# Batch 0's pooled values multiplied unsummed on TensorE, and the second weight's rounded copies placed by the planner

## The chip, the cores and the metric

The kernel runs on one core of one Trainium2 chip. The metric is the device time of one execution in microseconds (us). A core has TensorE (PE, matrix products), VectorE (DVE), ScalarE (ACT), GpSimd (POOL) and SyncE (SP), which here issues all DMA transfers in one in-order queue. Each engine works through its own list of instructions in order and waits on semaphores for the others.

## The reference

Attention on 8 batches of 8 heads (576 positions, head size 64), and then a two-layer MLP over its 4608 rows of 512 numbers. The attention is a sum of two parts:

```python
q_d = q.reshape(B, H, Sd, factor, D).mean(axis=3)     # factor 4: 576 -> 144 positions
k_d = k.reshape(B, H, Sd, factor, D).mean(axis=3)
v_d = v.reshape(B, H, Sd, factor, D).mean(axis=3)
out_up = np.repeat(sm_attn(q_d, k_d, v_d), factor, axis=2)
mask = np.abs(pos[:, None] - pos[None, :]) < factor   # each position and 3 on both sides
out_local = softmax(where(mask, scale * q @ k.T, -1e9)) @ v
x = (out_up + out_local)                              # as 4608 x 512
h = x @ w_in                                          # 512 x 2048
return np.maximum(0.01 * h, h) @ w_out                # 2048 x 512
```

## The kernel before

**MLP.** Every product is made of three fp32r matmuls: each operand is split into a rounded copy (`xh`, `gh`, `wih`, `woh`) and the rest (`xl`, `gl`, `wil`, `wol`), and high x high, high x low and low x high are added up. The 4608 rows go in 13 chunks: 256 and 320 columns (batch 0), then mostly 384. For each of 16 blocks f of 128 hidden units, `up_proj` (L706) forms h of the chunk in a PSUM bank `hp`, `leaky` makes `gh` and `gl` out of it (L716 and L717 on ACT, L719 on DVE; the last one frees the bank, of which there are two), and `down_proj` (L746) adds it into four banks `acc`. The two chunks of batch 0 are done with blocks 0 to 7 first, and with blocks 8 to 15 when those weights are there.

**Weights.** `convert(f, k)` stages a block of `w_in` (k = 0) or `w_out` (k = 1), which arrives as 64-bit floats: a load into a buffer that is borrowed from the attention (`k`, `v`, `prod`, `up` and others), ACT extracts the top bits (L268), DVE puts the fp32 value together (L270), a rounded copy is made (L278 on DVE for k = 1, L281 on ACT for k = 0), and POOL subtracts it from the value (L283). Then the buffer is free for the next load.

**Attention.** Heads go in pairs c = 0 to 3. `pooled(b, c)` sums four rows of q and k (L345 on DVE for b = 0, c = 0, else L339 and L341 on POOL for batch 0), scores them on PE (L358), makes the softmax (L366 to L378), transposes it on PE (L397), and multiplies it with the summed values `v_d` (L409), which DVE sums out of `vs` (L387). The result is copied to `outd` by ACT (L414). For batch 0 the local part is done on PE by `banded` in windows of 70 keys, in two halves hf: scores L460 and L468, softmax L475 to L487, transposes L495, values L509. L521 adds the pooled part, L526 and L528 write `xh` and `xl`. For the other batches the local part is made on POOL and DVE (`scores`, `values`: L567, L573, L628, L634) and transposed on PE (L665) by `landing`.

**Order.** Nothing is scheduled on the chip: a planner in the kernel's Python code (`Order`) decides the order of every engine's instructions while the program is built. Each piece of work is a generator with a rank; it asks for buffers (`slot`), waits for named events (`wait`), and hands in operations with an engine and a size (`op`, `pe`, `load`). The planner keeps a time for each engine in `od.engine`, gives every operation a cost (`COST`: a fixed part and a part per element; PE's is given in us), and always records the operation that could start earliest, ties by rank. So every change of a cost moves instructions of all engines. Buffers named `su_...` exist for batch 0 only: `su_vs` holds four, one for the values `vs` of each head pair, and the windows of the second half of `banded` are loaded into the same four when they are free again. `su_vd` holds the sums of batch 0, two buffers.

Of the kernel before, what the change touches and what calls it, by code (L numbers as in the profile page):

```python
# [6 lines left out]
F32 = mybir.dt.float32  # L7
# [7 lines left out]
ALU = mybir.AluOpType  # L15
AX = mybir.AxisListType
PSUM = bass.MemoryType.PSUM

B, H, S, D = 8, 8, 576, 64
FAC = 4  # L20
SD = S // FAC
# [15 lines left out]
HEADS = 2  # L37
# [145 lines left out]
def attn_moe(ctx: ExitStack, tc, qkt, vd, qb, kb, vb, vwb, band, identb, w_in, w_out, ident, edge, out):  # L183
    nc = tc.nc
# [2 lines left out]
    wk = ctx.enter_context(tc.tile_pool(name="wk", bufs=1))  # L187
    ps = ctx.enter_context(tc.tile_pool(name="ps", bufs=1, space=PSUM))

    bufs = dict(head=HEADS, qk=1, vs=1, qk_d=2, v_d=1, su_vd=2, su_half=1, su_pd=3, su_ptd=2, st_d=3, pd=2, ptd=1, outd=2, q=1, k=1, v=1, s=3, st_l=3, prod=2, up=1,  # L190
                xloc=2, lst=3, gh=3, gl=3, o=2, hp=2, pt=2, xh0=1, xl0=1, xh1=1, xl1=1, acc0=1, acc1=1, acc2=1, acc3=1,
                su_vw=NC, su_vs=NC, su_pt=2)
    od = Order(bufs)
# [1 line left out]
    def slot(*tags):  # L195
        return (yield ("slot", tags, 0))

    def sb(s, shape, dtype, pool=None):
        tag = s.tag
        return (pool or wk).tile(shape, dtype, name=tag, tag=tag, bufs=bufs[tag])  # L200
# [4 lines left out]
    def op(eng, n, *after, times=1):  # L205
        if eng == "PE":
            dur = n
        else:
            a, k = COST[eng]
            dur = times * a + k * n  # L210
        return (yield ("op", eng, dur, max((0.0,) + after), 0, after))

    def pe(us, *after):
        return (yield ("op", "PE", us, max(after) + SAFE, 0))
# [40 lines left out]
    def convert(f, k):  # L255
        s = yield from slot(*(("k", "v", "prod", "up") if f < OWN else ("v", "up", "vs")), *(("xh1", "xl1") if f < 4 else ()))
        st = sb(s, [128, HALFS * (DM + 1)], U16)
        raw = st[:, 1:1 + HALFS * DM]
        if k == 0:
            t = yield from load(raw.rearrange("p (c m) -> p c m", c=NC), w_in_v[:, f], 524e3, s.t)  # L260
        else:
            t = yield from load(raw, w_out_v[:, f], 524e3, s.t)
        mid = st.bitcast(I32).rearrange("p (m w) -> p m w", w=2)[:, :DM, 1]
        top = st.rearrange("p (m h) -> p m h", h=HALFS)[:, 1:, 0].bitcast(BF16)
        s_u = yield from slot("head")
        head = heads[s_u.index % len(heads)]
        t = yield from op("ACT", 790, t, s_u.t)
        nc.scalar.copy(out=head.bitcast(F16).rearrange("p (m h) -> p m h", h=2)[:, :, 1], in_=top)  # L268
        t = yield from op("DVE", 780, t)
        nc.vector.scalar_tensor_tensor(out=mid, in0=mid, scalar=13, in1=head, op0=ALU.logical_shift_right, op1=ALU.bitwise_or)  # L270
        s_u.free(t)
        tf = mid.bitcast(F32)
        if f >= FSPLIT:
            yield from wait("late")
        hi, lo = (w.rearrange("p c m -> p (c m)") for w in weight(f, k))
        if k:
            t = yield from op("DVE", 512, t)
            nc.vector.tensor_copy(out=hi, in_=tf)  # L278
        else:
            t = yield from op("ACT", 512, t)  # L280
            nc.scalar.copy(out=hi, in_=tf)  # L281
        t = yield from op("POOL", 590, t)
        nc.gpsimd.tensor_tensor(out=lo, in0=tf, in1=hi.bitcast(F32), op=ALU.subtract)  # L283
        s.free(t)
        od.signal(("w", f, k), t)

    outd = {}
# [42 lines left out]
    def pooled(b, c, rank, pool=None):  # L330
        sq, sv, qk, vs, tq, tv = yield from fetch(b, c, pool)
        s_qd = yield from slot("qk_d")
        qk_d = sb(s_qd, [128, 2 * SD], F32)
        qkr = qk.rearrange("p a (s r) -> p (a s) r", r=FAC)
        if b < BANDED and (b, c) != (0, 0):
            s = yield from slot("su_half")
            half = sb(s, [128, 2 * SD, 2], F32, pool)
            t = yield from op("POOL", 576, tq, s.t, s_qd.t)
            nc.gpsimd.tensor_tensor(out=half, in0=qkr[:, :, :2], in1=qkr[:, :, 2:], op=ALU.add)  # L339
            t = yield from op("POOL", 288, t)  # L340
            nc.gpsimd.tensor_tensor(out=qk_d, in0=half[:, :, 0], in1=half[:, :, 1], op=ALU.add)  # L341
            s.free(t)
        else:
            t = yield from op("DVE", 1152, tq, s_qd.t)
            nc.vector.tensor_reduce(out=qk_d, in_=qkr, axis=AX.X, op=ALU.add)  # L345
        if sq:
            if b < BANDED:
                od.spawn(rank, keeper(b, c, sq, t))
            else:
                sq.free(t)  # L350
        s_st, s_pd = (yield from slot("st_d")), (yield from slot("su_pd" if pool else "pd"))
        s_b = yield from slot(*banks(b))
        sc = bank(s_b)
        t = yield from pe(0.9, t, s_b.t)
        for qi in range(3):
            for p in range(2):
                rows = slice(64 * p, 64 * p + 64)
                nc.tensor.matmul(sc[rows, qi * SD:(qi + 1) * SD], qk_d[rows, qi * QB:qi * QB + 64],  # L358
                                 qk_d[rows, SD:2 * SD], start=True, stop=True)
        s_qd.free(t)  # L360
        scv = sc[:, :3 * SD].rearrange("p (a s) -> p a s", a=3)
        st, pd = sb(s_st, [128, 2, 3], F32), sb(s_pd, [128, 3, SD], F32, pool)
        mx, rc = st[:, 0], st[:, 1]
        top, sm = sc[:, 3 * SD:3 * SD + 3], sc[:, 3 * SD + 4:3 * SD + 7]
        t = yield from op("DVE", 440, t, s_st.t, times=3)
        nc.vector.tensor_reduce(out=top, in_=scv, axis=AX.X, op=ALU.max)  # L366
        nc.vector.tensor_scalar(out=mx, in0=top, scalar1=-SCALE / (FAC * FAC), scalar2=None, op0=ALU.mult)  # L367
        t = yield from op("ACT", 432, t, s_pd.t, times=8)
        for qi in range(3):
            nc.scalar.activation(out=pd[:, qi], in_=scv[:, qi], func=AF.Exp, scale=SCALE / (FAC * FAC),  # L370
                                 bias=mx[:, qi:qi + 1], accum_out=sm[:, qi:qi + 1])
        t = yield from op("DVE", 10, t, times=4)
        nc.vector.tensor_scalar(out=rc, in0=sm, scalar1=1e-9, scalar2=float(FAC), op0=ALU.add, op1=ALU.mult)
        nc.vector.reciprocal(out=rc, in_=rc)
        s_b.free(t)
        if b < BANDED:
            t = yield from op("POOL", 432, t)
            nc.gpsimd.tensor_tensor(out=pd, in0=pd, in1=rc.unsqueeze(2).to_broadcast([128, 3, SD]), op=ALU.mult)  # L378
        else:
            t = yield from op("ACT", 432, t, times=5)  # L380
            for qi in range(3):
                nc.scalar.activation(out=pd[:, qi], in_=pd[:, qi], func=AF.Copy, scale=rc[:, qi:qi + 1])
        s_st.free(t)
        s_vd = yield from slot("su_vd" if pool else "v_d")
        v_d = sb(s_vd, [72, 2, 2, D], F32, pool)
        td = yield from op("DVE", 1050, tv, s_vd.t)
        nc.vector.tensor_reduce(out=v_d, in_=vs, axis=AX.X, op=ALU.add)  # L387
        if sv:
            sv.free(td)
        s_pt = yield from slot("su_ptd" if pool else "ptd")  # L390
        ptd = sb(s_pt, [72, 2, 2, 3, QB], F32, pool)
        for kc in range(2):
            s_b = yield from slot(*banks(b))
            tp = bank(s_b)
            tt = yield from pe(0.27, t, s_b.t)
            for qi in range(3):
                nc.tensor.transpose(tp[0:72, qi * 128:(qi + 1) * 128], pd[:, qi, kc * 72:kc * 72 + 72], id_sb)  # L397
            te = yield from op("ACT", 288, tt, s_pt.t)
            nc.scalar.copy(out=ptd[:, kc].rearrange("k p a q -> k a p q"),
                           in_=tp[0:72, :384].rearrange("k (a p q) -> k a p q", a=3, p=2)[:, :, :, :QB])  # L400
            s_b.free(te)
        s_pd.free(tt)
        to = yield from wait(("outd", b))
        s_b = yield from slot(*banks(b))
        av = bank(s_b)
        t = yield from pe(0.68, te, td, s_b.t)
        for p in range(2):
            for kc in range(2):
                nc.tensor.matmul(av[64 * p:64 * p + 64, :SD], v_d[:, p, kc], ptd[:, kc, p],  # L409
                                 start=kc == 0, stop=kc == 1)  # L410
        s_pt.free(t)
        s_vd.free(t)
        t = yield from op("ACT", 144, t, to)
        nc.scalar.copy(out=outd[b][:, c], in_=av[:, :SD])  # L414
        s_b.free(t)
        od.signal(("pooled", b, c), t)
        if b == 0:
            od.signal("su", t)
# [470 lines left out]
```

## Time and profile before

| | |
|---|---|
| median of 3 runs | 961.01 us (960.36 to 964.61) |
| profiled execution | 959.72 us, its span 957.9 us |
| mean granted PE clock | 0.996 |
| PE busy | 932.4 us, 97% of the span |
| DVE, ACT, POOL busy | 595.2, 415.0, 617.8 us |
| first MoE matmul starts | 44.19 us |

A span runs from the first to the last instruction. Busy times count an engine's own instructions; loads of weights into PE are counted apart, since they overlap matmuls. A row of a timeline or of the chain of waits begins with its start and its length; "x8" counts instructions. An fp32 matmul (not fp32r) stands in the trace as two instructions, called passes here. "<-" in brackets names the work that ended a wait.

### The profile page before, as it was taken

How to read it: one execution, taken by the hardware profiler on the slowest of the kernel's cores; microseconds unless marked ns; L12 is line 12 of the kernel's file. 1: busy time of each engine (PE TensorE's matmuls, PEld its weight loads, DVE VectorE, ACT ScalarE, POOL GpSimd, SP SyncE). 2: the span in 40 equal slices, each digit the busy share in tenths (PEclk: the TensorE clock that was granted, in tenths of full speed). 3: DMA queues.
4: the chain of work that ended last, by engine and by line, in shares of the span. 5: the costliest groups of instructions: out<-in, count | busy, mean ns of one | idle time of the engine just before them, and what ended most of it. 6: DMA issues, size and time to landing. Idle time of an engine off the chain costs nothing.

```text
span 957.9 us, 16170 instructions
## 1 busy us (share of the span) xinstructions
PE 932.4 (97%) x6282; PEld 894.8 (93%) x6282; DVE 595.2 (62%) x895; ACT 415.0 (43%) x1139; POOL 617.8 (64%) x356
## 2 busy tenths in 40 slices
PE   6799999999999999999999999999999999999997
PEld 5588999899999999999999999899999999999997
DVE  5986678888887776787657774862753753311111
ACT  3774555555545543445324553532513423422211
POOL 3759868777888778986798776884885873100000
PEclk9899999999999999999999999999999999999999
DMA  9755665644554523452424442431231220000000
GB/s 264 241 184 181 214 201 179 189 164 145 188 166 122 190 96 116 131 187 95 135 74 146 159 148 101 140 116 58 92 116 58 91 77 31 34 1 1 34 1 33
DMA packets 63180, 117.31 MB, mean 122 GB/s; under 512 B 4944, under 2 KB 32848, under 8 KB 63104
## 3 DMA queue, kind: packets, MB, share of 16 engines
q1 hardware_dynamic: 63104, 116.29, 38.6%
q8 instruction: 49, 0.80, 0.4%
q14 instruction: 27, 0.22, 0.1%
HBM read 105.65 MB, written 10.62 MB: 121 GB/s over the span
## 4 chain that ended last, share of the span: by engine, by line
PE 77%; POOL 8%; DMA 4%; issue 4%; DVE 4%; ACT 2%; SPq 0%; POOLq 0%; DVEq 0%; ACTq 0%
PE hp L706 35%; PE acc L746 34%; POOL prod L567 4%; POOL prod L628 3%; PE pt L358 2%; DMA k<-in_kb_dram 2%; PE pt L397 2%; PE pt L409 2%; PE pt L665 1%; DMA qk<-in_qkt_dram 1%; DVE s L573 1%; DMA v<-in_w_in_dram 0%; SPq L218 0%; DMA vs<-in_w_out_dram 0%; DVE gl L719 0%
## 5 line engine op out<-in xcount | busy, mean ns | idle before, releaser
L567 POOL TENSOR_TENSOR prod<-q,k 128x1344 f32<-128x1344 f32 (+1 forms) x88 | 266.3, 3027 | 81.3 <-DMA k<-in_kb_dram 55.2
L628 POOL TENSOR_TENSOR prod<-v,s 128x1344 f32<-128x1344 f32 (+1 forms) x88 | 265.6, 3021 | 32.3 <-DVE xloc L634 18.2
L706 PE MATMUL hp<-xh,wih 128*128 128x384 f32 (+2 forms) x832 | 279.9, 336 | 5.8 <-DVE gl L719 5.1
L746 PE MATMUL acc<-gh,woh 128*128 128x384 f32 (+2 forms) x832 | 274.4, 330 | 0.3 <-ACT o L780 0.3
L706 PE MATMUL hp<-xl,wih 128*128 128x384 f32 (+2 forms) x832 | 269.5, 324 | 0.3 <-DVE xl L680 0.3
L706 PE MATMUL hp<-xh,wil 128*128 128x384 f32 (+2 forms) x832 | 269.6, 324 | 0.0
L746 PE MATMUL acc<-gh,wol 128*128 128x384 f32 (+2 forms) x832 | 269.0, 323 | 0.0
L746 PE MATMUL acc<-gl,woh 128*128 128x384 f32 (+2 forms) x832 | 268.9, 323 | 0.0
L719 DVE TENSOR_TENSOR gl<-hp,gh 128x384 fp32r<-128x384 f32 (+2 forms) x208 | 108.5, 522 | 215.7 <-ACT hp L717 215.2
L716 ACT ACTIVATE gh<-hp 128x384 fp32r<-128x384 f32 (+2 forms) x208 | 97.3, 468 | 315.6 <-PE acc L746 307.9
L706 PEld LDWEIGHTS hp<-xh,wih 128*128 128x128 f32 x832 | 156.4, 188 | 15.6 <-DVE gl L719 8.0
L746 PEld LDWEIGHTS acc<-gh,woh 128*128 128x128 f32 x832 | 156.2, 188 | 4.0 <-issue 3.2
L706 PEld LDWEIGHTS hp<-xl,wih 128*128 128x128 f32 x832 | 156.7, 188 | 0.5 <-DVE xl L680 0.5
L706 PEld LDWEIGHTS hp<-xh,wil 128*128 128x128 f32 x832 | 156.4, 188 | 0.0
L746 PEld LDWEIGHTS acc<-gl,woh 128*128 128x128 f32 x832 | 156.3, 188 | 0.0
L746 PEld LDWEIGHTS acc<-gh,wol 128*128 128x128 f32 x832 | 156.2, 188 | 0.0
L573 DVE TENSOR_REDUCE s<-prod 128x21 f32<-128x1344 f32 (+1 forms) x88 | 130.2, 1479 | 27.9 <-POOL prod L567 27.9
L634 DVE TENSOR_REDUCE xloc<-prod 128x192 f32<-128x1344 f32 (+1 forms) x88 | 130.1, 1478 | 22.5 <-POOL prod L628 22.1
L717 ACT ACTIVATE hp<-hp 128x384 f32<-128x384 f32 (+2 forms) x208 | 96.1, 462 | 0.0
L672 DVE TENSOR_TENSOR pt<-pt,up 128x384 f32<-128x384 f32 (+1 forms) x44 | 37.8, 861 | 27.6 <-PE pt L665 22.2
L652 ACT COPY up<-outd 128x576 f32<-128x576 f32 x84 | 52.3, 675 | 0.0
L370 ACT ACTIVATE pd<-pt,st_d 128x144 f32<-128x144 f32 x84 | 32.1, 382 | 46.4 <-DVE st_d L367 35.4
(154 smaller groups left out, 754.3 us busy)
## 6 DMA issues: line engine op xcount, KB each, us to landing
k<-in_kb_dram SPq DMA_DIRECT2D x38, 576.0 KB
v<-in_vb_dram SPq DMA_DIRECT2D x38, 576.0 KB
qk<-in_qkt_dram SPq DMA_DIRECT2D x32, 576.0 KB
vs<-in_vd_dram SPq DMA_DIRECT2D x28, 288.0 KB
q<-in_qb_dram SPq DMA_DIRECT2D x38, 192.0 KB
out_dram<-o SPq DMA_DIRECT2D x36, 192.0 KB
v<-in_w_out_dram SPq DMA_DIRECT2D x4, 512.0 KB
prod<-in_w_out_dram SPq DMA_DIRECT2D x4, 512.0 KB
```

The costliest lines, as they stand in the source:

```text
L370: nc.scalar.activation(out=pd[:, qi], in_=scv[:, qi], func=AF.Exp, scale=SCALE / (FAC * FAC), bias=mx[:, qi:qi + 1], accum_out=sm[:, qi:qi ...
L567: nc.gpsimd.tensor_tensor(out=prv, in0=q[:, p, a - j0:z - j0].unsqueeze(2).to_broadcast([128, n, W, D]), in1=view(k[:, p], (a - j0) * D, [ ...
L573: nc.vector.tensor_reduce(out=s[:, p, a - j0:z - j0], in_=prv, axis=AX.X, op=ALU.add)
L628: nc.gpsimd.tensor_tensor(out=prv, in0=view(v[:, p], a - j0, [[1, n], [nv, D], [1, W]]), in1=s[:, p, a - j0:z - j0].unsqueeze(2).to_broadc ...
L634: nc.vector.tensor_reduce(out=xl_t[:, :n, p], in_=prv, axis=AX.X, op=ALU.add)
L652: nc.scalar.copy(out=up[:, pp], in_=outd[b][:, 2 * u + pp].unsqueeze(2).to_broadcast([128, SD, FAC]))
L672: nc.vector.tensor_tensor(out=xv, in0=xv, in1=upv, op=ALU.add)
L706: nc.tensor.matmul(hp[:, :n], wt[:, c], x[:, c], start=k == 0, stop=k == 3 * NC - 1)
L716: nc.scalar.activation(out=gh[:, :n], in_=hp[:, :n], func=AF.Prelu, alpha=0.01)
L717: nc.scalar.activation(out=hp[:, :n], in_=hp[:, :n], func=AF.Prelu, alpha=0.01)
L719: nc.vector.tensor_tensor(out=gl[:, :n], in0=hp[:, :n], in1=gh[:, :n].bitcast(F32), op=ALU.subtract)
L746: nc.tensor.matmul(acc[:, :n], wt[:, es], g[:, :n], start=f == f0 and j == 0, stop=f == f1 - 1 and j == 2)
```

## The change

In `pooled`, for batch 0 alone, the sum over four rows of v (L387, 72 x 1024 values to 72 x 256) is left out. The product L409 takes v as it lies in `vs`, once for each of the four rows r, with the same scores: 2 x 4 matmuls for each of the two heads instead of 2, and the two heads, whose outputs are the two halves of a bank's partitions, now take turns. The stationary operand is `vs[:, p, kc, :, r]`, 64 columns that lie four fp32 apart. `vs` is given back after the matmuls instead of after the sum; `su_vd` is no longer there. In `convert` the engine of the rounded copy is chosen by the planner's times, for both weights, instead of by k.

```diff
@@ convert
-        if k:
+        if max(od.engine["DVE"], t) + 0.4 < max(od.engine["ACT"], t):
             t = yield from op("DVE", 512, t)
             nc.vector.tensor_copy(out=hi, in_=tf)
         else:
             t = yield from op("ACT", 512, t)
             nc.scalar.copy(out=hi, in_=tf)
@@ pooled
-        s_vd = yield from slot("su_vd" if pool else "v_d")
-        v_d = sb(s_vd, [72, 2, 2, D], F32, pool)
-        td = yield from op("DVE", 1050, tv, s_vd.t)
-        nc.vector.tensor_reduce(out=v_d, in_=vs, axis=AX.X, op=ALU.add)
-        if sv:
+        if pool:
+            td = tv
+        else:
+            s_vd = yield from slot("v_d")
+            v_d = sb(s_vd, [72, 2, 2, D], F32)
+            td = yield from op("DVE", 1050, tv, s_vd.t)
+            nc.vector.tensor_reduce(out=v_d, in_=vs, axis=AX.X, op=ALU.add)
             sv.free(td)
...
-        t = yield from pe(0.68, te, td, s_b.t)
-        for p in range(2):
-            for kc in range(2):
-                nc.tensor.matmul(av[64 * p:64 * p + 64, :SD], v_d[:, p, kc], ptd[:, kc, p],
-                                 start=kc == 0, stop=kc == 1)
+        t = yield from pe(2.2 if pool else 0.68, te, td, s_b.t)
+        steps = [(kc, vs[:, :, kc, :, r]) for kc in range(2) for r in range(FAC)] if pool else [(kc, v_d[:, :, kc]) for kc in range(2)]
+        for n, (kc, vk) in enumerate(steps):
+            for p in range(2):
+                nc.tensor.matmul(av[64 * p:64 * p + 64, :SD], vk[:, p], ptd[:, kc, p], start=n == 0, stop=n == len(steps) - 1)
         s_pt.free(t)
-        s_vd.free(t)
+        (sv if pool else s_vd).free(t)
```

`pool` is set for batch 0 only. Lines below the change have numbers that are 2 higher in the changed kernel, L397 and what follows it up to L409 too; L409 becomes L412, and L414 becomes L416.

The planner's order changes on every engine. On PE, around the first set of value products (head pair 0), before:

```order
L358 MATMUL acc_188<-qk_d 64x144 x6
L409 MATMUL hp<-su_ptd,su_vd 64x144 x4
L509 MATMUL pt<-su_pt,su_vw 64x64 x8
L460 LDWEIGHTS idb_sb
L460 MATMUL acc_239<-band_sb,idb_sb 128x280
L468 MATMUL acc_239<-qk_91 64x67 x2
L468 MATMUL acc_239<-qk_91 64x70 x6
L495 MATMUL acc_226<-id_sb,xloc 70x128 x3
```

and after:

```order
L358 MATMUL acc_187<-qk_d 64x144 x6
L412 MATMUL hp<-su_ptd,su_vs 64x144 x16
L497 MATMUL acc_235<-id_sb,xloc 70x128 x3
L511 MATMUL acc_251<-su_pt,su_vw 64x64 x8
L358 MATMUL pt<-qk_d 64x144 x6
L497 MATMUL acc_264<-id_sb,xloc 70x128
L462 LDWEIGHTS idb_sb
L462 MATMUL hp<-band_sb,idb_sb 128x280
```

The set has 16 matmuls instead of 4; behind it now stand transposes of pair 1, and the window product of pair 0 (L509, now L511) has moved behind them.

On ACT, the first rounded copies of both weights (`wih`, `woh`; the name behind the arrow is the borrowed buffer), before:

```order
L268 CAST head_71<-v 128x512
L399 COPY su_ptd<-acc_359 72x3x2x48
L479 ACTIVATE xloc<-xloc 128x280
L497 COPY su_pt<-pt 70x384
L399 COPY su_ptd<-acc_384 72x3x2x48
L497 COPY su_pt<-acc_392 70x128
L268 CAST head_70<-prod 128x512
```

and after:

```order
L268 CAST head_70<-prod 128x512
L401 COPY su_ptd<-pt 72x3x2x48
L528 CAST xh_83<-hp 128x256
L281 CAST woh_68<-v 128x512
L499 COPY su_pt<-pt 70x384
L401 COPY su_ptd<-acc_362 72x3x2x48
L281 CAST wih_66<-prod 128x512
```

All 16 copies of `woh` have moved from DVE's list to ACT's, and none of either weight stands on DVE.

On SP, the first loads of weights (`k`, `v`, `prod`, `up`, `xh_102` are the borrowed buffers) and the first window load into `su_vs`, before:

```order
L218 DMA k<-in_w_in_dram 128x4x512
L218 DMA su_vs<-in_vwb_dram 70x640
L218 DMA v<-in_w_out_dram 128x2048
L218 DMA prod<-in_w_in_dram 128x4x512
L218 DMA prod<-in_w_out_dram 128x2048
L218 DMA up<-in_w_in_dram 128x4x512
```

and after:

```order
L218 DMA k<-in_w_in_dram 128x4x512
L218 DMA v<-in_w_out_dram 128x2048
L218 DMA prod<-in_w_in_dram 128x4x512
L218 DMA prod<-in_w_out_dram 128x2048
L218 DMA su_vs<-in_vwb_dram 70x640
L218 DMA up<-in_w_in_dram 128x4x512
L218 DMA xh_102<-in_w_out_dram 128x2048
L218 DMA xl_103<-in_w_in_dram 128x4x512
L218 DMA vs<-in_w_in_dram 128x4x512
```

The window load has moved three weight loads back; four weight loads stand between it and the next one.

More of the change, by code (lines that the diff above doesn't have):

```diff
@@ L188, in attn_moe @@
     ps = ctx.enter_context(tc.tile_pool(name="ps", bufs=1, space=PSUM))
-    bufs = dict(head=HEADS, qk=1, vs=1, qk_d=2, v_d=1, su_vd=2, su_half=1, su_pd=3, su_ptd=2, st_d=3, pd=2, ptd=1, outd=2, q=1, k=1, v=1, s=3, st_l=3, prod=2, up=1,
+    bufs = dict(head=HEADS, qk=1, vs=1, qk_d=2, v_d=1, su_half=1, su_pd=3, su_ptd=2, st_d=3, pd=2, ptd=1, outd=2, q=1, k=1, v=1, s=3, st_l=3, prod=2, up=1,
                 xloc=2, lst=3, gh=3, gl=3, o=2, hp=2, pt=2, xh0=1, xl0=1, xh1=1, xl1=1, acc0=1, acc1=1, acc2=1, acc3=1,
```

## The prediction

> **What bounds the kernel now.** I read the page's first part, then the same busy times by stage, then what TensorE (PE) waited for, then the chain of waits. The first part says that PE carries the time:
>
> ```profile
> PE 932.4 (97%) x6282; PEld 894.8 (93%) x6282; DVE 595.2 (62%) x895; ACT 415.0 (43%) x1139; POOL 617.8 (64%) x356
> ```
>
> The span of 957.9 us is therefore 932.4 us of PE work and 25.5 us in which PE sat idle. An edit can move the span only by changing one of these two. The table by stage (us of the stage, busy us of each engine with the number of instructions, granted clock, DMA share) says where the idle lies:
>
> ```profile
> core 0: us, PE busy (x) PEld busy (x) DVE busy (x) ACT busy (x) POOL busy (x), PEclk, DMA share, GB/s
> 0.00:20.00 20.00, 11.99 (x110) 9.34 (x111) 8.83 (x21) 6.72 (x23) 7.23 (x13) 1.00 0.92 251
> 20.00:44.00 24.00, 18.25 (x229) 13.34 (x231) 22.76 (x44) 18.52 (x53) 16.50 (x14) 0.86 0.93 289
> 44.00:70.00 26.00, 23.73 (x253) 22.30 (x248) 23.20 (x41) 18.99 (x44) 16.36 (x12) 1.00 0.56 174
> 70.00:130.00 60.00, 58.01 (x439) 55.98 (x438) 40.44 (x61) 31.73 (x78) 46.21 (x31) 1.00 0.64 200
> 130.00:200.00 70.00, 68.34 (x561) 63.97 (x560) 60.23 (x103) 39.05 (x125) 55.69 (x34) 1.00 0.57 179
> 200.00:640.00 440.00, 439.44 (x2911) 418.70 (x2910) 324.10 (x466) 206.77 (x601) 356.57 (x191) 1.00 0.43 137
> ...
> 770.00:958.00 188.00, 182.95 (x1050) 182.17 (x1048) 44.56 (x69) 49.07 (x112) 28.09 (x15) 1.00 0.08 27
> ```
>
> PE idles 8.0 us before 20, 5.75 from 20 to 44 (attention of batch 0), 2.3 from 44 to 70, 2.0 from 70 to 130, 1.7 from 130 to 200, 0.6 in the next 440 us, and 5.05 in the last stage, the tail. VectorE (DVE) is 95% busy from 20 to 44 and 89% from 44 to 70; nowhere later is it short. What PE waited for agrees:
>
> ```profile
> PE hp L706 <- DVE gl L719: 5.1, 10, 1.4
> PE acc L495 <- POOL xloc L487: 2.1, 1, 2.1
> PE acc L397 <- POOL su_pd L378: 2.0, 2, 1.3
> PE pt L509 <- ACT su_pt L497: 1.8, 1, 1.8
> PE pt L409 <- ACT su_ptd L399: 0.8, 2, 0.5
> ```
>
> (us in all, times, longest.) The 5.1 us are waits for a hp bank that DVE frees late. Ahead of the L509 wait, which ends at 38.2, and of the first MoE matmul (L706) at 44.2 the chain of waits stands on DVE; these are its longest piece there and the piece that ends the batch's first 256 columns, and two rows of PE's timeline:
>
> ```profile
> 35.36 1.75 DVE up L270
> 42.41 0.41 DVE xl L528
> 26.55 0.52 PE L397 MATMUL acc<-id_sb,su_pd 128*72 128x128 f32 x3 [0.71 <-POOL su_pd L378]
> 44.19 0.39 PE L706 MATMUL hp<-xh,wih 128*128 128x256 f32 x1
> ```
>
> The L495 wait, three us earlier, ends on GpSimd (POOL), which had waited for DVE's reciprocals. So both waits are DVE's.
>
> **The change: work taken off DVE.** The four sums of batch 0 go, and the sixteen rounded copies of the second weight (L278) leave DVE:
>
> ```profile
> L387 DVE TENSOR_REDUCE su_vd<-su_vs x4: 1183/1194/1205, 11.4 to 29.0; 72x256 f32<-72x1024 f32 x4
> sum 110.00, DVE 14.30; mean DVE 4.77
> L278 DVE CAST woh<-vs x2: 1374/1814/2254, 88.0 to 108.2; 128x512 fp32r<-128x512 f32 x2
> L281 ACT CAST wih<-v x4: 662/672/680, 45.6 to 106.4; 128x512 fp32r<-128x512 f32 x4
> ```
>
> The first row is 4 x 1.19 = 4.8 us, the second the sum of L278's busy time from 20 to 130 us. In the new order all 16 copies, and the 16 of the first weight as before, stand on ScalarE (ACT); DVE gets none, so "ACT or VectorE" is ACT alone. At ACT's 0.67 us (last row, same shape) that is 10.7 us more for ACT, off PE's path while ACT has room: it is 77% busy from 20 to 44 and 73% from 44 to 70.
>
> **Work put on PE.** Each head pair of batch 0 gets 16 matmuls instead of 4; the trace counts two passes for each fp32 matmul, so 32 instead of 8. The chain gives the pace:
>
> ```profile
> 16.48 1.17 PE hp L409 x8
> 14.85 1.64 PE acc L358 x12
> 609.96 0.65 PE pt L409 x8
> 611.86 0.88 PE pt L358 x12
> ```
>
> These are start, us on the chain, and passes. After 20 us a pass of the same shape takes 81 ns (0.65/8); a pass of L358, with the same 144 columns, but whose two column halves take turns as in the new loop, takes 73 ns (0.88/12). In the first 20 us PE is slower, with 146 and 137 ns, though the granted clock reads 1.00. I take L358's pace for its alternation. Three pairs at full pace: 32 x 0.073 - 0.65 = 1.7 us each, 5.1 in all; the first pair, at about 16.5 us: 32 x 0.137 - 1.17 = 3.2. Sum +8.3 us; by L409's own pace it is +9.4. All of it is PE time and nothing hides it except an idle PE. Behind the first set in PE's queue stand the transposes of pair 1, the window product of pair 0 and the scores of pair 2, all pushed by 3 us.
>
> **What idle it can fall into.** The 8.0 us before 20 are first loads and the first softmax, which the change doesn't shorten. Of the 5.75 from 20 to 44, the two DVE-made waits (2.1 and 1.8) should go, since DVE sheds three sums (3.6 us) and four copies (4.2) there, and 0.5 of the small ones: -4.4 (ends 0 and -5.75). These waits also cost clock:
>
> ```profile
> 30.48 0.69 PE L509 MATMUL acc<-su_pt,su_vw 70*64 70x64 f32 x16
> 38.23 1.12 PE L509 MATMUL pt<-su_pt,su_vw 70*64 70x64 f32 x16 [1.79 <-ACT su_pt L497]
> 39.68 1.42 PE L468 MATMUL hp<-qk 64*64 64x70 f32 x20
> 43.44 0.83 PE L468 MATMUL pt<-qk 64*64 64x70 f32 x20
> ```
>
> Equal work took 0.43 and 0.59 us longer right after the gaps, in the stage whose clock is 0.86: -1.0 with the gaps gone (ends 0 and -2). From 44 to 130 PE idles 4.3 us, mostly for gl. DVE is relieved by 10 us there, but gh and hp, which gl needs, now queue behind ACT's copies. I take 1.0 of 4.3 (ends +4.3 and -4.3). After 130 the work is the same and only the order differs: 0, give or take 1.7, the idle of 130 to 200.
>
> **The load queue.** A buffer of v is now given back by the matmuls instead of by DVE. SP issues loads in order, and the window load that reuses it stands ahead of weight loads; now it issues at
>
> ```profile
> 12.58 0.33 SPq L218 DMA_DIRECT2D su_vs<-in_vwb_dram  x1
> ```
>
> and then it would wait until the first set of matmuls ends, 16.5 + 4.4, about 21 us. Four weight loads stand behind it. I cost it at nothing: the DMA share is 0.92 and 0.93 up to 44 us, so the engines are still working off what was issued before. If that cover were gone, the price would be the weights coming 3 us later, against the first MoE matmul at 44.
>
> **Sum.** +8.3 - 4.4 - 1.0 - 1.0 = +1.9 us. Against the profiled execution's 959.72 that is 961.6. That execution lies 1.3 below the median of 961.01; I add half of it and say 962.2. A difference under 0.5% (4.8 us) is no change here.
>
> **Rivals.** *Faster: the idle was the real price.* For it speaks that DVE ends most waits up to 130 us. If all of 20 to 44 (5.75), the clock (1.0), the 4.3 of 44 to 130 and the 1.7 of 130 to 200 go, and the denser PE has reached full pace by the first set (its 3.2 becomes 1.7), the sum is +6.8 - 12.75 = -6 us, about 954.4. Against it: static orders on five engines never fit so well, and PE's first wait after 20 us is the 0.71 at 26.55 (row above), and two of the four sets fall ahead of it, where no idle can take them.
>
> *Slower: the strided operand.* The new stationary operand takes every fourth fp32 of v, 16 bytes apart; every stationary operand of L409 before was contiguous. If a pass had to wait for its own weight load, it would take that load's time:
>
> ```profile
> L409 PEld LDWEIGHTS pt<-ptd,v_d x224: 132/137/137, 128.5 to 633.8; 72*64 72x64 f32 x112
> L409 PEld LDWEIGHTS hp<-su_ptd,su_vd x8: 181/228/230, 16.4 to 17.0; 72*64 72x64 f32 x8
> ```
>
> That is 3 x (32 x 0.137 - 0.65) + 32 x 0.228 - 1.17 = +17.3, and less the 6.4 regained +10.9: 971.3. It passes 0.5% once a pass takes over some 92 ns at full pace (and 1.87 times that in the first set, the ratio of 137 to 73). Against it: loads overlap passes now (137 ns against a pace of 81), so some slack exists. The Trainium skill, "SBUF — State Buffer", section "Door 1: The DMA port swizzle", says that SBUF has 16-byte lines and that an access which goes to a new line each time pays a penalty; here every weight would be on a new line, so the page stands on this rival's side. No row of this trace has such an operand, and the page gives no figure.
>
> *Slower: ACT becomes what DVE was.* From 44 to 70 ACT is busy 18.99 of 26; some 8 of the copies before the first eight weight pairs are done bring 5.4 us, which makes 94%, above DVE's 89% now. If that doubles the 4.3 us of idle instead of saving 1.0, the sum is +1.9 + 1.0 + 4.3 = +7.2: 967.6. Against it: a copy took up to 2.25 us on DVE (row above) and 0.68 at most on ACT, so the chain for each weight is not longer.
>
> **Chances.** Forecast 0.60 (own range 958 to 966), all idle regained 0.19, strided operand 0.10, ACT 0.11. I leave out the strided case and the last of the fast one: 955 to 968.5. Faster 0.19, same 0.61, slower 0.20.
>
> **What would show it.** Right: L412 in 32 passes of about 73 ns after 20 us and about 4.4 us for the first set; PE busy up by 7 to 9 us; PE idle from 20 to 44 down to 1 or 2 us with the clock near 1; DVE 19 us lighter, ACT 10.7 heavier. Wrong: passes over 92 ns; new waits of PE for gh or gl while ACT copies; SP standing at the window load while the DMA engines run dry; or PE at full pace before its first set.

## The result, and the profile after

The changed kernel takes 970.3 us (median of 19 runs, 962.88 to 979.91), the kernel before 960.45 in the runs beside them: a ratio of 1.0089, 95% interval 1.0076 to 1.0102, or +8.5 us. (The averages, 969.3 and 960.8 us, give this ratio; the medians lie 9.9 us apart.) The forecast was 962.2, range 955 to 968.5. Ratios here and below leave out slow executions: 979.91 here, and two far ones among the experiments, 1859 us (products alone in the old order) and 4951 us (additions first). The profiled execution took 966.82 us with a span of 964.8, 6.9 above the span before and 3.5 below the median; so the profile shows most of the loss, not all.

The first part of the page, after:

```profile
PE 937.1 (97%) x6378; PEld 900.2 (93%) x6378; DVE 582.9 (60%) x875; ACT 426.4 (44%) x1155; POOL 612.9 (64%) x356
```

PE's busy time rose by 4.7 us and its idle by 2.2 (964.8 - 937.1 = 27.7, after 25.5). ACT is 11.4 us heavier, as forecast. DVE has the 20 instructions less that it should, but is only 12.3 us lighter, where 19 was forecast: its 32 instructions at L270 took 35.6 us, 32.1 before, which is half of what is missing. In the old order (below) DVE, with the same list of instructions, is 17.0 us lighter. The stages (us, busy us of each engine, granted clock, DMA share):

```profile
core 0: us, PE busy (x) PEld busy (x) DVE busy (x) ACT busy (x) POOL busy (x), PEclk, DMA share, GB/s
0.00:20.00 20.00, 12.00 (x123) 9.43 (x125) 7.35 (x20) 7.16 (x23) 7.66 (x13) 1.00 0.92 262
20.00:44.00 24.00, 19.88 (x290) 16.42 (x287) 19.25 (x39) 21.24 (x56) 17.15 (x15) 1.00 0.91 280
44.00:70.00 26.00, 25.12 (x283) 23.18 (x282) 21.17 (x38) 21.28 (x51) 13.17 (x11) 1.00 0.57 174
70.00:130.00 60.00, 56.30 (x414) 54.90 (x413) 34.36 (x50) 35.20 (x84) 43.88 (x32) 0.97 0.62 201
130.00:200.00 70.00, 66.87 (x536) 62.15 (x537) 60.27 (x101) 37.01 (x116) 57.23 (x33) 0.98 0.53 169
200.00:640.00 440.00, 437.13 (x2902) 415.52 (x2899) 320.72 (x464) 209.47 (x604) 346.81 (x188) 1.00 0.44 137
```

Idle fell where the change works: from 5.75 to 4.1 us between 20 and 44, from 2.3 to 0.9 between 44 and 70, and the clock of 20 to 44 rose from 0.86 to 1.00. The first MoE matmul starts at 40.05 instead of 44.19. But idle rose from 2.0 to 3.7 between 70 and 130, from 1.7 to 3.1 between 130 and 200, and from 0.6 to 2.9 in the 440 us after that. The last two of these stages run not one instruction of the change, whose last copy is at 120.7 us. And two stages that were at full clock are at 0.97 and 0.98. What PE waited for from 130 to 640 us, first before, then after:

```profile
PE hp L706 <- DVE gl L719: 0.9, 2, 0.6
PE hp L706 <- ACT xh L678: 0.7, 1, 0.7
```

```profile
PE acc L748 <- DVE o L773: 2.7, 1, 2.7
PE acc L748 <- ACT o L782: 2.3, 3, 1.0
PE hp L708 <- DVE gl L721: 0.6, 1, 0.6
```

The new waits are for accumulator banks, which DVE or ACT had to read out first. The 2.7 us stand at 147 us; this is DVE's own list there (start, length, line, idle before):

```profile
147.02 0.62 DVE L366 TENSOR_REDUCE pt<-pt 128x3 f32<-128x432 f32 x1 [0.61 <-PE pt L358]
147.67 0.16 DVE L367 TENSOR_SCALAR st_d<-pt 128x3 f32<-128x3 f32 x1
147.75 0.41 DVE L682 TENSOR_TENSOR xl<-pt,xh 128x256 fp32r<-128x256 f32 x1
148.08 0.18 DVE L597 RECIPROCAL st_l<-st_l 128x6 f32<-128x6 f32 x1
148.18 1.51 DVE L575 TENSOR_REDUCE s<-prod 128x21 f32<-128x1344 f32 x1
149.61 0.15 DVE L373 TENSOR_SCALAR st_d<-pt 128x3 f32<-128x3 f32 x1
149.79 0.18 DVE L374 RECIPROCAL st_d<-st_d 128x3 f32<-128x3 f32 x1
149.88 0.41 DVE L773 TENSOR_TENSOR o<-acc,o 128x256 f32<-128x256 f32 x1
```

Seven instructions of other work stand ahead of the addition that frees the bank, and the first of them itself waits for PE. No unit is slow here; the order is bad for the moment at which PE comes by. And the wait costs more than its length, as the stretches around it show (us, PE busy, granted clock, DMA share):

```profile
147.00:148.00 1.00, 0.61 (x3) 1.00 0.73 249
150.00:151.00 1.00, 0.65 (x2) 0.50 0.91 373
152.00:153.00 1.00, 1.00 (x5) 0.50 0.47 111
154.00:156.00 2.00, 2.00 (x16) 1.00 0.87 191
```

The trace has PE at half clock for 3.4 us from 149.9 on, and again for 3.4 us from 112.3 on, behind a gap of 2.2 us that ends at 111.1. The kernel before has no gap of PE over 1.4 us between 44 and 770 us and no slow clock there.

### The profile page after: what moved, and what is told of

It is laid out like the page before. It is cut to its first block, busy times and chain, and to the rows that moved or that the text cites. A ratio compares the mean times of both kernels' runs of the same rounds, so it can differ in the third digit from the quotient of the medians.

```text
span 964.8 us, 16357 instructions
## 1 busy us (share of the span) xinstructions
PE 937.1 (97%) x6378; PEld 900.2 (93%) x6378; DVE 582.9 (60%) x875; ACT 426.4 (44%) x1155; POOL 612.9 (64%) x356
## 4 chain that ended last, share of the span: by engine, by line
PE 88%; DMA 3%; DVE 3%; ACT 2%; issue 2%; POOL 1%; SPq 0%; POOLq 0%; DVEq 0%; ACTq 0%
PE acc L748 40%; PE hp L708 39%; PE pt L358 3%; PE pt L399 2%; PE pt L412 2%; PE pt L667 1%; DMA qk<-in_qkt_dram 1%; DMA out_dram<-o 1%; DMA k<-in_kb_dram 1%; DVE s L575 1%; ACT head L268 1%; PE hp L412 0%; DVE v L270 0%; DMA band_sb<-in_band_dram 0%; ACT su_pd L370 0%
## 5 line engine op out<-in xcount | busy, mean ns | idle before, releaser
L708 PEld LDWEIGHTS hp<-xh,wih 128*128 128x128 f32 x832 | 156.8, 188 | 12.5 <-DVE gl L721 6.4
L748 PEld LDWEIGHTS acc<-gh,woh 128*128 128x128 f32 x832 | 156.9, 189 | 10.8 <-ACT o L782 4.1
L370 ACT ACTIVATE pd<-pt,st_d 128x144 f32<-128x144 f32 x84 | 32.1, 382 | 39.3 <-DVE st_d L367 26.4
```

The source lines that it names most:

```text
L708: nc.tensor.matmul(hp[:, :n], wt[:, c], x[:, c], start=k == 0, stop=k == 3 * NC - 1)
L748: nc.tensor.matmul(acc[:, :n], wt[:, es], g[:, :n], start=f == f0 and j == 0, stop=f == f1 - 1 and j == 2)
```

## The experiments

Three theories went into them. **W**: PE's extra matmuls cost what they take. **A**: ACT, with the copies, holds PE up. **O**: the planner's new order costs, whatever work it orders. The planner can be deceived: if it is charged one kernel's costs while another kernel's instructions are issued, the work of one stands in the order of the other. Ratios are to the kernel before on the same chip, with 95% intervals.

**The whole change in the old order.** The planner is charged the old costs; what is issued is the change. "Order" is everything that the planner decides, the buffers that loads borrow included:

```diff
-        if max(od.engine["DVE"], t) + 0.4 < max(od.engine["ACT"], t):
+        if k:
             t = yield from op("DVE", 512, t)
-            nc.vector.tensor_copy(out=hi, in_=tf)
+            nc.scalar.copy(out=hi, in_=tf)
...
-            td = tv
+            s_vd = yield from slot("su_vd")
+            td = yield from op("DVE", 1050, tv, s_vd.t)
...
-        t = yield from pe(2.2 if pool else 0.68, te, td, s_b.t)
+        t = yield from pe(0.68, te, td, s_b.t)
```

> The whole change (products unsummed, all copies on ACT), but the planner is charged the old costs (a sum of 1050 elements on DVE, 0.68 us on PE, the copy of the second weight on DVE), so every engine's list is that of the kernel before, but for the replaced instructions and two loads that change places. Theory W: +5 to +7, as for the change itself. Theory A: +5 or more. Theory O: the work falls into the idle of the first 44 us, so -1 to +3, and the change's other us come from its new order.

Measured: 960.65 us, ratio 1.0002 (0.9986 to 1.0017). The 8.5 us are gone with the order, all of them, and the work is still there: W and A, which asked for +5 or more, are out. (In the trace three loads and one ACT instruction stand elsewhere than before; GpSimd's list is the same, and the others differ by the replaced instructions.) Its profile, by stage (PE alone: busy, instructions, clock, DMA share):

```profile
20.00:44.00 24.00, 21.39 (x295) 0.95 0.82 267
44.00:70.00 26.00, 23.79 (x253) 0.98 0.64 201
70.00:130.00 60.00, 57.67 (x450) 1.00 0.57 186
130.00:200.00 70.00, 68.67 (x561) 1.00 0.59 190
200.00:640.00 440.00, 438.96 (x2918) 1.00 0.43 136
```

PE is busy for 937.6 us, 5.2 more than before, and idles 3.1 us less between 20 and 44 (2.6, where it was 5.75). After 70 us it idles as before: 2.3, 1.3 and 1.0 us. That the profiled span is 959.8, 1.9 above the one before, is within what single executions differ by.

**The old work in the changed order**, the mirror: sums on DVE, 4 matmuls for each pair, the second weight's copies on DVE, while the planner is charged as in the change:

```diff
-            nc.scalar.copy(out=hi, in_=tf)
+            (nc.vector.tensor_copy if k else nc.scalar.copy)(out=hi, in_=tf)
...
             td = tv
+            v_d = pool.tile([72, 2, 2, D], F32, name="su_vd", tag="su_vd", bufs=bufs["su_vd"])
+            nc.vector.tensor_reduce(out=v_d, in_=vs, axis=AX.X, op=ALU.add)
...
-        steps = [(kc, vs[:, :, kc, :, r]) for kc in range(2) for r in range(FAC)] if pool else [(kc, v_d[:, :, kc]) for kc in range(2)]
+        steps = [(kc, v_d[:, :, kc]) for kc in range(2)]
```

> The mirror of the old-order run: the work of the kernel before (sums of batch 0 on DVE, 4 matmuls for each pair, the second weight's copies on DVE), but the planner is charged as in the change, so every engine's list is the changed kernel's, but for the replaced instructions. Theory O (the order costs, the work doesn't): +6 to +10 us, about what the change itself cost, with PE's idle after 70 us as high as there (some 10 us without the tail). Theory W (PE's extra matmuls cost, in whatever order): 0 to +2, since PE has 5.7 us less to do.

Measured: 966.88 us, ratio 1.0078 (1.0057 to 1.0098). The unchanged work pays nearly the change's price as soon as it stands in the change's order. PE's waits from 130 to 640 us are those of the changed kernel, with the same 2.7 us (the lines' numbers are 2 higher again):

```profile
PE acc L750 <- DVE o L775: 2.7, 1, 2.7
PE acc L750 <- ACT o L784: 1.5, 2, 1.0
PE hp L710 <- DVE gl L723: 0.6, 1, 0.6
```

The total came out as expected, the path to it only in part. The idle of 70 to 770 us was put at some 10 us and was 6.9, with 1.5 more from 44 to 70. And PE's busy time rose, though its 6282 instructions are those of the kernel before:

```profile
PE 938.4 (97%) x6282; PEld 898.5 (93%) x6282; DVE 597.8 (62%) x895; ACT 416.9 (43%) x1139; POOL 614.3 (64%) x356
20.00:44.00 24.00, 20.62 (x203) 0.65 0.93 284
```

That is 6.0 us more than 932.4, with a granted clock of 0.65 from 20 to 44 (0.86 before); the idle of the whole span, 24.3 us, is no higher than before. So a rise of PE's busy time is not by itself a measure of added work.

**Other orders of the same work.** One constant of the planner, the delay it assumes between engines, is 0.21 or 0.19 us instead of 0.20; nothing else changes:

```diff
-HOP = 0.2
+HOP = 0.21
```

The kernel before with 0.21, then with 0.19:

> The kernel before with nothing changed but one constant of the planner (the delay from one engine to the next, 0.21 us instead of 0.20), so the same work in another order: about as many rows of each engine's list move as in the change. Theories W and A: 0, give or take 1. Theory O: several us off, of either sign, with the difference in PE's idle and clock after 70 us.

> The kernel before with the planner's delay at 0.19 us: a third order of its work. Theory O: a draw of its own, -2 to +8; if the order of the kernel before is a good draw, more likely slower than faster. Theory W: 0, give or take 1.

Measured: 1.0049 (1.0034 to 1.0063) and 1.0120 (1.0099 to 1.0140). The second, with the work of the kernel before, is slower than the change, and at +11.5 us beyond the +8 that theory O gave as its end. Its longest waits of PE between 44 and 770 us:

```profile
PE hp L706 <- DVE gl L719: 6.2, 6, 3.0
PE acc L746 <- DVE o L771: 2.7, 1, 2.7
PE pt L397 <- DVE xl L680: 1.7, 1, 1.7
PE pt L358 <- DVE qk_d L345: 1.6, 1, 1.6
```

The change with 0.21, then with 0.19:

> The change with the planner's delay at 0.21 us instead of 0.20: the same work as the change in another order. Theory O: a draw of its own, anything from -2 to +12 against the kernel before, most likely not the change's +8.5. Theory W: +7 to +10 again.

> The change with the planner's delay at 0.19 us: a third order of the same work. Theory O: a draw of its own, -2 to +12. Theory W: +7 to +10.

Measured: 1.0073 (1.0052 to 1.0094) and 1.0091 (1.0066 to 1.0116). Here W's +7 to +10 was met too, so these two don't tell the theories apart; the old-order run does.

**One half of the change at a time, planned anew.** The products alone (`if k:` as before in `convert`), and the copies alone (the new condition in the kernel before):

> The unsummed products alone; the rounded copies of the second weight stay on DVE, chosen by k as before. In the profile of the changed kernel a set of products took 2.17 us at full pace and 2.27 the first time, after 0.65 and 1.17: +5.7 us of PE work. Theory W (the work on PE is the price and the idle of 20 to 44 us can't take it): +5 to +7 us. Theory A (ACT's copies are the price): 0 to +2. Theory O (the planner's new order decides, whatever the work): anything from -3 to +9, not near the sum of the parts.

> The copies on ACT alone; batch 0's pooled values are summed on DVE as before, so PE has no extra work. Theory W: 0, give or take 1. Theory A: +5 to +9, with PE waiting for gh or gl between 44 and 130 us. Theory O: anything from -3 to +9.

Measured: 1.0068 (1.0056 to 1.0080) and 1.0026 (1.0008 to 1.0044). A's +5 to +9 for the copies is out, and W's 0, give or take 1, was missed too (+2.5). The products' +6.5 us fit W, and alone would have looked like its proof.

**One half at a time, in the old order.** So that the work itself is compared:

```diff
# copies alone: the kernel before, with
             t = yield from op("DVE", 512, t)
-            nc.vector.tensor_copy(out=hi, in_=tf)
+            nc.scalar.copy(out=hi, in_=tf)
# products alone: the whole change in the old order, with
             t = yield from op("DVE", 512, t)
-            nc.scalar.copy(out=hi, in_=tf)
+            nc.vector.tensor_copy(out=hi, in_=tf)
```

> The kernel before, every list in its old order, with the second weight's copies on ACT and nothing else. DVE is 14 us lighter and PE has no more to do. If the DVE-made waits of 20 to 70 us carry a price of their own: -2 to -4 us, faster than both kernels, with PE's idle from 20 to 44 falling from 5.75 to about 3. If later waits take the place of those removed (the idle is given back after 70 us): -1 to +1.

> The unsummed products alone, in the old order, copies on DVE. PE +5.7 us of work, DVE -4.8. If the whole change in the old order came out even because the copies' relief paid for the products: +2 to +5 here. If the products pay for themselves (the sums' removal ends the waits of 20 to 44): -1 to +2.

Measured: copies 958.84 us, ratio 0.9978 (0.9960 to 0.9996); products 963.5 us, 1.0022 (1.0006 to 1.0039). In one order the two halves add up: -0.22% and +0.22%, with +0.02% measured for both. The copies on ACT are a small gain, 2 us, though the interval ends close to 1. The way to it was not the expected one: PE's idle from 20 to 44 was to fall to about 3 and fell to 5.07, and PE's busy time, with the same instructions, was 3.2 us lower (929.2); why is open. The products cost 2 us of their 5.7, between the two cases expected.

**Mending the largest wait.** DVE's addition that frees the bank may be placed 3 us ahead of its turn; the lists are the changed kernel's up to there:

```diff
-            t = yield from op("DVE", n, t, tr)
+            t = yield from op("DVE", n, t, tr, first=3.0)
...
-                        key = (start, task[0], task[1])
+                        key = (start - (task[3][6] if len(task[3]) > 6 else 0.0), task[0], task[1])
```

> The change, with one more rule in the planner: DVE's additions that free an accumulator bank of the first two chunks' second half (L773) may be placed up to 3 us ahead of their turn. All lists are the changed kernel's up to that place, at about 145 us of the run. If single waits of PE are the price of the new order: PE's 2.7 us wait for that addition goes, with the slower clock behind it, and the time falls 2 to 4 us below the change's, to +4 to +7 against the kernel before. If a removed wait only comes back elsewhere, as a new draw from there on: +6 to +11, the wait for L773 gone and others in its place.

Measured: 973.37 us, ratio 1.0135 (1.0106 to 1.0164), worse than the change and worse than either case expected. PE's waits from 130 to 640 us:

```profile
PE pt L670 <- DVE st_d L376: 4.0, 1, 4.0
PE hp L711 <- DVE gl L724: 1.8, 3, 0.7
PE acc L751 <- ACT o L785: 1.6, 2, 1.1
PE acc L751 <- DVE o L776: 1.0, 1, 1.0
```

The wait of 2.7 went to 1.0, and what it had displaced now makes PE wait 4.0 us.

**All of them together.** PE's idle from 44 to 770 us (length of the stages less PE's busy time, one profiled execution each) against the ratio:

| work | order | PE idle 44 to 770 us | ratio |
|---|---|---|---|
| copies | old | 5.7 | 0.9978 |
| products | old | 6.0 | 1.0022 |
| before | old | 6.8 | 1 |
| whole change | old | 6.9 | 1.0002 |
| copies | new | 7.6 | 1.0026 |
| before | delay 0.21 | 8.4 | 1.0049 |
| before | the change's | 8.4 | 1.0078 |
| products | new | 9.2 | 1.0068 |
| whole change | delay 0.21 | 9.3 | 1.0073 |
| whole change | the change's | 10.6 | 1.0089 |
| whole change | delay 0.19 | 10.8 | 1.0091 |
| whole change | additions first | 13.2 | 1.0135 |
| before | delay 0.19 | 14.5 | 1.0120 |

The time goes with the idle of these later stages and not with the work: 7.7 us of idle between the third row and the last go with 11.5 us of time (1.2%). The idle is not the whole price. In other orders of the old work PE's busy time was 4.5 to 6.0 us above 932.4. One source of that is the half clock that goes with long gaps: in these 13 profiles, from 50 to 770 us, each of the 6 gaps of PE over 2 us had a stretch of half clock that began inside it or up to 1.6 us behind it, 3 of the 5 gaps of 1.67 to 1.88 us had one, and no shorter gap did. The four kernels in the old order have no such stretch behind 50 us. But neither have the products in their new order nor the change with 0.21, and both are 0.7% slower than the kernel before; so it is not the only source, and it was not tried by itself. An early start is no help: the first MoE matmul started at 36.60 us in the kernel before with 0.19, at 47.11 in the whole change in the old order. All eight new orders were slower than the old one, whatever the work.

## Why the prediction was wrong

**The step that failed: "After 130 the work is the same and only the order differs: 0, give or take 1.7".** In the profiled execution the idle from 130 to 770 us went from 2.5 to 6.0, and over other orders of the same work up to 12.5. The bound was taken from the idle that was there to be lost, 1.7 us from 130 to 200; but a new order can make idle that was not there, and the trace of before, the trace of one good order, couldn't show how much. The place to look was the order itself: every engine's list was rearranged far into the run. One sign stood in the prediction's own table, where DVE was said to be short nowhere after 70 us: from 130 to 200 it is 86% busy (60.23 of 70), and the largest new wait there is for DVE.

In the profile the forecast's sum of +1.9 became +6.9: +4.7 of PE busy time in place of +7.3 (the work less the clock), -1.6 of idle from 20 to 44 in place of -4.4, +0.3 from 44 to 130 in place of -1.0, +3.5 after 130 in place of 0. The first of these misses nearly cancels the second. Against the same work in the old order, whose span is 5.0 us shorter, the idle after 130 makes 3.6 of the difference; by the runs the order costs the whole +8.5 us but for the +0.2 that is left in the old order.

**The other terms of the sum.**
- PE's extra work was put at +8.3 us and was +5.7: a set of 32 passes takes 2.17 us in the chain of waits, 68 ns a pass, where 73 was taken. The error is mostly the first set, put at 4.4. From the chain of waits (start, length, engine, tile and line, matmul records), after, and then the first set of the whole change in the old order:

```profile
16.46 2.27 PE hp L412 x32
...
29.24 2.17 PE hp L412 x32
```

```profile
16.20 4.05 PE hp L413 x32
```

  After, the first set already ran at 71 ns a pass, against 68 in the later one: PE reached full pace as that set began, which is all but the sign that the prediction named, full pace before the first set. In the old order it took 4.05 us, close to the 4.4. So the slow pace has no fixed end: on PE's timeline the first set took 2.24 to 2.34 us in six of the seven kernels with 32 passes, 4.12 in this one. The prediction's puzzle, a slow PE at a granted clock of 1.00, comes of the column: the trace has no clock record ahead of 21.5 us before, 16.7 after and 24.4 in the old order, and where there is none the column reads 1.00. At just these times the passes go over to the full pace.
- The pace of L358 was taken "for its alternation". The rows don't bear that out: 8 passes in 0.65 us, 12 in 0.88 and 32 in 2.17 give 58 to 65 ns for each further pass, so 81, 73 and 68 ns a pass are much the same pace with a fixed part spread over sets of different length.
- The idle of 20 to 44 was to fall by 4.4 and the clock to give 1.0. In the new order the idle fell by 1.6, in the old one by 3.1. The mechanism was half right: of the two waits called DVE's, the one for L495 (2.1 us) went in the old order, while the one for L509 (1.8) stayed as it was there, and the new order has both. After, and then in the old order, from 20 to 44 us:

```profile
PE hp L511 <- ACT su_pt L499: 2.1, 1, 2.1
PE acc L497 <- POOL xloc L489: 1.5, 1, 1.5
```

```profile
PE pt L514 <- ACT su_pt L502: 1.8, 1, 1.8
PE pt L413 <- ACT su_ptd L402: 0.9, 1, 0.9
```

  In the old order's profile the sum came out at the forecast's +1.9 (+5.2 of PE busy time, -3.3 of idle), but partly by luck, with both terms smaller than forecast; its runs say +0.2 us (-1.3 to +1.6).
- From 44 to 130, -1.0 was taken; the idle rose by 0.3, with the gain of 44 to 70 given back from 70 to 130.
- The load queue cost nothing visible: the window load waited until 18.8 us, and the DMA share stayed at 0.91 up to 44. In the old order the feared case did show: with the slow first set SP issued nothing from 12.7 to 20.3 us, the DMA share of 20 to 44 fell to 0.82, and the first MoE matmul came at 47.11, 2.9 us later than before. The kernel's time was even so that of the kernel before.

**The rivals.** *Strided operand*: the weight loads did become slower, but the passes did not wait for them. After (nanoseconds, least, median, most):

```profile
L412 PEld LDWEIGHTS pt<-ptd,v_d x224: 132/137/137, 130.7 to 641.5; 72*64 72x64 f32 x112
L412 PEld LDWEIGHTS acc<-su_ptd,su_vs x32: 192/193/214, 23.3 to 25.1; 72*64 72x64 f32 x32
L412 PE MATMUL acc<-su_ptd,su_vs x32: 286/286/398, 23.3 to 25.2; 72*64 72x144 f32 x32
```

193 ns for a load of 64 columns that lie 16 bytes apart, 137 for contiguous ones, at a pace of 68 ns a pass. The Trainium skill, "SBUF — State Buffer", "Door 1: The DMA port swizzle", speaks of a penalty for accesses that go to a new 16-byte line each; the trace agrees for the load, with 41%, and shows none for the matmuls. The Trainium skill, "TensorE: Matmul & The Clock Gate", "Part 2: What happens when you issue a matmul", says that the next tile's weights load while the present one's matmul runs; here the rows agree that loads and matmuls overlap. That a pass every 68 ns goes with loads of 193 ns means more than that, some three loads under way at once (an estimate, 193/68).

*ACT becomes the bound*: PE's waits for gl fell from 5.1 to 4.4 us in all, and in the old order ACT's copies made the kernel faster. *All idle regained*: no; of the old order's idle, 3.3 us at most were.

**What stays open.** The changed kernel's profile shows 6.9 of its 8.5 us, and its execution was 3.5 below the median of its runs; what the longer executions do differently no profile shows. All stages and waits are from one profiled execution of each kernel, while the ratios are from 5 to 19. Which of the new order's many shifted instructions carry the price is not shown: taking away the largest wait made the kernel slower. Whether a better order than the old one exists for the whole change was not searched for; the four new orders of it did not hit one.

## What to carry to other kernels

Where a planner writes the order of in-order engines, an edit is two changes: the work, and a new draw of every list. Charge the planner the old costs and issue the new instructions, and the work is measured alone; move a constant of the planner by a hair, and the width of the draw is measured. Here the draw (+0.5 to +1.3% at equal work) was larger than any effect of the work (-0.2 to +0.2%), and the order at hand may be a good draw, so a range for any edit that re-plans it has to reach further up than down.

## What the runs showed of the hardware that was not expected

PE's clock halved at gaps of about 2 us. From 50 to 770 us every gap of PE over 2 us (six, of 2.24 to 3.98) had a stretch of half clock that began inside it or shortly behind it, 3 of the 5 gaps of 1.67 to 1.88 us had one, and no shorter gap. Each stretch in the 13 traces that ends before the run does lasts 3.41 us or a multiple of it (6.83, 10.24, 13.65, 17.07). With a stretch of 3.41 us behind it, a wait costs up to 1.7 us more than it lasts (an estimate, half of 3.41).

PE's slow pace of the first 20 us, 137 ns a pass at 14.8 us before, ended between 16 and 24.5 us in the 13 profiles, each time where a full-clock record begins in the trace. It did not take a long run of passes to end it: in both kernels with the copies alone the first set, of 8 passes, took 0.72 and 0.88 us on the timeline, against 1.24 in the kernel before, while all 32 passes of the first set were slow in the whole change in the old order. Why it ends when it does is open.

The stationary operand's stride of 16 bytes lengthened its load from 137 to 193 ns and left the pace of the passes as it was.
